# Two reorderings in a fused attention and GEGLU kernel: three up steps placed later, two weight loads placed earlier

## The chip, the cores and the metric

The kernel runs on one core of a Trainium2 chip. The metric is the time of one execution in microseconds as the device reports it; where several executions were made, their median is given. A profiled execution records when each instruction of each engine began and ended. Its *span* runs from the first to the last of them; the execution's time is somewhat longer than the span.

## The reference

One transformer block with its two branches side by side. Sequence 2048, width 448, 16 heads of 28, feed-forward width 1792; all inputs are bfloat16.

```python
def _A_ref(x, wqkv, wo):                      # sliding-window attention, W = 256
    qkv = ((x @ wqkv).reshape(B, S, 3, H, Dh)).transpose(2, 0, 3, 1, 4)
    q, k, v = qkv[0], qkv[1], qkv[2]
    scores = einsum("bhqd,bhkd->bhqk", q, k) * (Dh ** -0.5)
    mask = (i - j >= 0) & (i - j < 256)
    p = softmax(where(mask, scores, -1e9))
    return einsum("bhqk,bhkd->bhqd", p, v).transpose(0, 2, 1, 3).reshape(B, S, D) @ wo

def _B_ref(x, w_gate, w_up, w_down):
    return (gelu(x @ w_gate) * (x @ w_up)) @ w_down

xn = _layernorm(x)
return x + _A_ref(xn, ...) + _B_ref(xn, ...)
```

## The kernel before

**Blocks and stages.** The 2048 tokens are handled in four blocks of 512 (`qb` 0 to 3). Each block has two stages. In the first, `attention(qb, plan)` makes the scores of the block in ten *score steps*; in the second, `gated(...)` computes the gate and up products of the feed-forward branch. The ten score steps leave TensorE room, and a list written out by hand, `plan`, says what it does in each of them besides: plan[i] belongs to step i, counted from 0. So plan[5] is the sixth step, and plan[9] the last one.

**The fillers.** A filler is a Python generator, and `(u, 3)` in the plan means: draw three times from `u`, and each draw emits a piece of work. In block 3, `d = gen_down(2)` computes the output rows of block 2 (down projection and output projection, PSUM tiles `po`, one matmul over 448 columns for each draw) and `u = gen_up(3, (1, ..., 6), (4, 6))` computes up products of block 3 ahead of the second stage, for the pairs 1 to 6. A *pair* p is feature tiles p and p + 7. Each draw from `u` is one of seven *chunk steps* of a pair (`chunk`, L453): two matmuls of 64 rows by 512 columns, one in the upper and one in the lower half of the array. After the seventh step of a pair its two results are copied from PSUM (`ue`) to `hT` in SBUF: both by VectorE (L473), or one by VectorE and one by ScalarE for the pairs 4 and 6.

**A score step** (L640 to L678) does, in this order: at step 4 and step 6 the product with V of the heads of groups 0 and 1 (`pv`, PSUM tiles `ov`, L624), whose two halves are then copied by ScalarE (L608) and added up by VectorE (L609); the masks of the step before (VectorE, L572); the scores of this step (`sc`, L652); their exponential (ScalarE, L656); the plan's entries. "sums" and "inverse" in the plan belong to the softmax: VectorE transposes and takes reciprocals, and after an "inverse" GpSimd multiplies (L591). `pv` for groups 2 and 3 follows in the second stage, after gate pair 0.

**PSUM.** There are eight banks of 512 float32 columns. Four belong to the scores: in the first stage one tile `sc` of four banks (`score_pool(1)`), in the second two tiles `gt` of two banks for the gate (`score_pool(2)`). The other four, `b0` to `b3`, are single banks for everything else (`ue`, `u`, `po`, `ov`, `pq`, `pv`). They are handed out by a list:

```python
    def take(name, cols=QB, tag=None):
        tag = tag or spare[0]
        spare.remove(tag)
    ...
    def give(*tiles):
        for ps in tiles:
            spare.append(held.pop(id(ps))[0])
```

So the bank that has been in the list longest comes first. `give` stands where the code has emitted the last reader; the bank's next writer still waits until that reader has run. A draw that begins a pair takes two banks and holds them until the seventh step's copies.

**Block 3, the plan's steps around the change.** plan[0] and plan[1] draw 21 times from `u`: pairs 1, 2 and 3 whole. plan[2] to plan[4] draw from `d`. plan[5] draws once from `d`, which ends the output rows of two token tiles (L408 to L414, two `po` banks given back), then seven times from `u` (pair 4), and then three more times. plan[6], plan[7] and plan[8] draw from `d`, and plan[9] draws the rest of `u`.

**Block 0, loads.** Nearly all loads are issued from one queue, SyncE's. `ahead3` (L778) issues, in this order: four transposes and swaps of x, the gate columns of the pairs 0 to 2 (`load_ffn(wg, ..., slice(0, 3))`, two DMAs, one for each half of the array), the last four x tiles (L787), the up columns of the pairs 5 and 6 (two DMAs), the gate columns of the pairs 3 to 6 (two DMAs), then the output weights `wo` (L793, L794) and the down weights `wd` (L797). A new DMA of this queue waits for the completion of the eighth one before it, as they share eight semaphores in turn. The last four x tiles are first read in block 1, by `stat(12)` on VectorE. The gate columns of pair 3 are first read in block 0's second stage, by the fourth gate product, and the up columns of pair 5 by the only two up products that this stage has in block 0, those of the pairs 5 and 6 (pairs 0 to 4 were made ahead).

**ScalarE's queue in block 0's second stage** has the gelus of the gate pairs (L496), and between those of pairs 4 and 5 three DMA issues (`o_collect`, L351), which wait for GpSimd's multiplications.

Of the kernel before, what the change touches and what calls it, by code (L numbers as in the profile page):

```python
# [27 lines left out]
def kernel(  # L28
# [38 lines left out]
    wg = const.tile([P, 7, F // 2], bf16, name="wg")  # L67
    wu = const.tile([P, 7, F // 2], bf16, name="wu")
# [3 lines left out]
    def rows(w, c0, n):  # L72
        return w[c0 * P:(c0 + n) * P, :].rearrange("(c p) n -> p c n", p=P)

    def load_ffn(dst, w, pairs):

        wv64 = w.rearrange("(c p) (h n) -> p c h n", p=64, h=2)
        ns = slice(pairs.start * P, pairs.stop * P)  # L80
        for hi in range(2):
            nc.sync.dma_start(out=dst[64 * hi:64 * hi + 64, :, ns], in_=wv64[:, :, hi, ns])  # L82
# [25 lines left out]
    masks = const.tile([P, 3, 4, 64], bf16, name="masks")  # L108
# [56 lines left out]
    def norm(t):  # L165
        xn = work.tile([P, 4, P], bf16, name="xn", bufs=4)
        xf = xn[:, :, :].rearrange("p a b -> p (a b)")
        both = ((0, D, 0), (D, 64, 384))
        for lo, n, src in both if t > 3 else both[:1]:
            nc.vector.tensor_scalar(out=xf[:, lo:lo + n], in0=x_sb[:, t, src:src + n], scalar1=mv_all[:, t, 0:1],  # L170
                                    scalar2=rstd_all[:, t:t + 1], op0=ALU.subtract, op1=ALU.mult)
        xns[t] = xn

    def dma_transp(t):

        nc.sync.dma_start_transpose(out=xnT[:, :, t * P:(t + 1) * P], in_=xns.pop(t)[:, :, :].rearrange("p a b -> p (a b)"))
# [100 lines left out]
    def fill_pads(last):  # L277


        def put(dst, src, n, lo):  # L280

            src = src.rearrange("p (j d) -> p j d", d=Dh)[:, :, lo:]
            if n == 4:
                nc.gpsimd.tensor_copy(out=dst[:, 12:16, Dh:32], in_=src[:, :, 24:28])
            src = src[:, :, 0:24].rearrange("p j (g i) -> p g j i", i=8)[:, :, :, 0:4]
            nc.gpsimd.tensor_copy(out=dst[:, 0:12, Dh:32].rearrange("p (g j) i -> p g j i", j=4), in_=src)

        if not last:
            for c in range(3):
                k = wraw[:, c, D + 12 * Dh:2 * D]  # L290
                put(wqp[:, c, :, :], k, 4, 0)
                put(wkp[:, c, :, :], k, 3, 4)
            return
        put(w3p[0:64, :, :], w3k[0:64, :], 4, 0)
        put(w3p[64:128, :, :], w3k[64:128, :], 3, 4)
        nc.gpsimd.memset(w3p[64:128, 12:16, :], 0.0)
# [131 lines left out]
    def new_hT(qb):  # L428
        hT = blk.tile([P, NF, QB], bf16, name="hT", tag="hT")
        hTs[qb] = hT  # L430

    def swap(qb, t=None, n=4):

        t0 = P * (4 * qb if t is None else t)
        to = t0 - qb * QB + ring(qb).start
        for hi in range(2):
            nc.sync.dma_start(out=xsw[64 * hi:64 * hi + 64, :, to:to + n * P],
                              in_=xnT[64 - 64 * hi:P - 64 * hi, 0:3, t0:t0 + n * P])

    def swap_weights():  # L440

        for hi, src in enumerate((wqp, wkp)):
            nc.sync.dma_start(out=wsq[64 * hi:64 * hi + 64], in_=src[64 - 64 * hi:P - 64 * hi, 0:3])
# [334 lines left out]
    def ahead3():  # L778
        for t in (5, 6, 7):
            norm(t)  # L780
            dma_transp(t)
        swap(1, 4, 2)
        swap(1, 6, 2)
        fill_pads(False)
        swap_weights()
        load_ffn(wg, B_w_gate, slice(0, 3))
        nc.sync.dma_start(out=x_sb[:, 12:16, :], in_=xv[:, 12:16, :])  # L787
        load_ffn(wu, B_w_up, slice(5, 7))
        load_ffn(wg, B_w_gate, slice(3, 7))
        wo_v = A_wo.rearrange("(g j d) n -> j d g n", g=4, j=4)  # L790
        tail = A_wo[14 * Dh:, :].rearrange("(t i) n -> i t n", i=4)
        for j, (t0, n) in enumerate(SLOTS):
            nc.sync.dma_start(out=wo[32 * j:32 * j + Dh, 0:n, :], in_=wo_v[j][:, 0:n])  # L793
            nc.sync.dma_start(out=wo[32 * j + Dh:32 * j + 32, 0:n, :], in_=tail[:, t0:t0 + n])  # L794
        for k in range(0, NF, 4):
            n = min(4, NF - k)
            nc.sync.dma_start(out=wd[:, k:k + n, :], in_=rows(B_w_down, k, n))  # L797

    for qb in range(NB):
        if qb in (1, 3):  # L800
            tc.mark_branch_hint_location("general", hint="LikelyTaken",
                                         engines=[mybir.EngineType.DVE if qb == 1 else mybir.EngineType.PE])
        early = ()
        if qb == 0:
            new_hT(0)
            early = (0, 1, 2, 3, 4)
            u = chain(gen_qk((1, 2, 3), {1: (3, pvs[3]), 2: (2, pvs[2])}), gen_up(0, (1, 2, 3, 0, 4), (3, 4)))
            w = gen_pairs(1, (("v", 0), ("v", 2), ("k", 0), ("k", 1), ("k", 2)))
            plan = [[(u, 2), ahead, (u, 1)], [lambda: v_dense(2, pvs[2]), (u, 2), ahead2, (u, 1)],
                    [lambda: spare.append(spare.pop(1)), (u, 2), ahead3, (u, 4)], [lambda: stat(8), (u, 11)],  # L810
                    [lambda: stat(9), (u, 7), lambda: stat(10), (u, 7), lambda: fill_pads(True)], ["sums", (u, 7)],
                    ["inverse", "scale", (w, 11)], [(w, 10)],
                    [lambda: stat(11), (w, 7), lambda: rstd(8, 4), "sums", "inverse", (w, 7)]]
        else:
            d = gen_down(qb - 1)
            if qb < 3:
                u = gen_pairs(qb + 1, (("v", 0), ("k", 0), ("v", 2), ("k", 1), ("k", 2)))
                plan = [[(d, 14)], [(d, 11)], [(d, 11)], [(u, 7)], [(d, 18)], ["sums", (u, 7), "inverse"], [(u, 11)],
                        [lambda: q_last(qb + 1, nc.vector.tensor_copy), (d, 6), "sums"], [(d, 2), "inverse", (d, 10)],
                        [(u, 9), "masks", (u, 1)]]  # L820
                plan[3] = [(d, 1), (u, 7)]
                if qb == 2:
                    plan[0], plan[2] = [(d, 13)], [(d, 10)]
                if qb == 1:
                    for i, j in enumerate((0, 1, 2, 4)):
                        plan[j].insert(0, lambda t=12 + i: stat(t))
                    plan[4].append(lambda: rstd(12, 4))
                    plan[1] = plan[1][:1] + [lambda: q_last(1, nc.vector.tensor_copy), (d, 8)]
                    plan[2] = plan[2][:1] + [(d, 12), lambda: collect(1)]
                    plan[4].append(lambda: deliver(1))  # L830
            else:
                new_hT(3)
                early = (1, 2, 3, 4, 5, 6)
                u = gen_up(3, early, (4, 6))
                plan = [[(u, 12)], [(u, 9)], [(d, 12)], [(d, 10)], [(d, 12)], [(d, 1), (u, 7), "sums", (u, 3)], [(d, 12), "inverse"],
                        ["sums", "inverse", (d, 12)], [(d, 12)], [(u, 10), "masks", (u, 1)]]
        if qb in (1, 2):
            swap(qb + 1)
        score_pool(1)
        rest, after, flush = attention(qb, plan)  # L840
        nc.scalar.preload_act_table(ACT.Gelu_apprx_tanh)
        score_pool(2)
        if qb not in hTs:
            new_hT(qb)

        def hook(f):
            after(f)
            if qb in (1, 2) and f == 0:
                collect(qb + 1)
            if f == (8, 2, 2, 6)[qb]:  # L850
                o_collect(qb, nc.sync if qb else nc.scalar)
            if f == (12, 4, 4, 6)[qb]:
                o_deliver(qb)
                o_finish(qb)
            if qb == 0 and f == 6:
                nc.gpsimd.tensor_copy(out=wo[64:128, 3, :], in_=wo[0:64, 3, :])
            if qb in (1, 2) and f == 10:
                deliver(qb + 1)
            t = ({0: 8, 4: 9, 8: 10, 10: 11} if qb == 0 else {4: 12, 6: 13, 8: 14, 10: 15} if qb == 1 else {}).get(f)
            if t is not None:  # L860
                norm(t)
                dma_transp(t)

        gated(qb, early, rest, flush, hook)
        if qb < NB - 1:
            nc.scalar.preload_act_table_set("natural_log_exp_and_others")
# [156 lines left out]
```

## Time and profile before

| | us |
|---|---|
| median of 3 runs | 215.34 |
| lowest, highest | 215.28, 216.34 |
| profiled execution, its time | 216.02 |
| profiled execution, its span | 214.2 |
| TensorE matmul busy | 207.8 |
| VectorE, ScalarE, GpSimd busy | 157.7, 131.6, 48.6 |

The stages of the span, from the chain of waits: block 0's scores run to about 37.3 us, its gate and up products to 52.8, block 1 to 103.7, block 2 to 153.7. Block 3's score steps run from there to 183.0, its gate and up products to 196.5, and the last output rows to 210.4. The granted TensorE clock was 0.998 of full speed over the span.

In the views, PE is TensorE's matmuls, PEld its weight loads (which overlap the matmuls), DVE VectorE, ACT ScalarE, POOL GpSimd, SPq the queue of SyncE that issues DMAs. L456 is line 456. The chain of waits follows the work that ended last backwards: at each step to what released it, or to the instruction before it on the same engine. As long as it stays on PE, TensorE had no gap; where it leaves PE, TensorE waited. Ends of matmuls are modelled, so starts are the safer numbers.

### The profile page before, as it was taken

How to read it: one execution, taken by the hardware profiler on the slowest of the kernel's cores; microseconds unless marked ns; L12 is line 12 of the kernel's file. 1: busy time of each engine (PE TensorE's matmuls, PEld its weight loads, DVE VectorE, ACT ScalarE, POOL GpSimd, SP SyncE). 2: the span in 40 equal slices, each digit the busy share in tenths (PEclk: the TensorE clock that was granted, in tenths of full speed). 3: DMA queues.
4: the chain of work that ended last, by engine and by line, in shares of the span. 5: the costliest groups of instructions: out<-in, count | busy, mean ns of one | idle time of the engine just before them, and what ended most of it. 6: DMA issues, size and time to landing. Idle time of an engine off the chain costs nothing.

```text
span 214.2 us, 6428 instructions
## 1 busy us (share of the span) xinstructions
PE 207.8 (97%) x2722; PEld 101.9 (48%) x2722; DVE 157.7 (74%) x355; ACT 131.6 (61%) x123; POOL 48.6 (23%) x86
## 2 busy tenths in 40 slices
PE   7999999999999999999999999999999999999992
PEld 2433444445444445444445445444445444544992
DVE  7899988999767985796536987494483889569531
ACT  4699588555777977423777887523676776766000
POOL 5287658350100220041000211032000022006001
PEclk9999999999999999999999999999999999999999
DMA  6999579969410101003521001001000101000111
GB/s 186 267 218 230 107 169 238 215 199 214 109 47 26 42 16 29 8 5 65 74 73 46 24 0 30 19 0 34 12 3 3 44 3 42 9 0 0 26 44 49
DMA packets 23993, 15.67 MB, mean 73 GB/s; under 512 B 9208, under 2 KB 23832, under 8 KB 23960
## 3 DMA queue, kind: packets, MB, share of 16 engines
q1 hardware_dynamic: 22918, 14.87, 31.6%
q8 instruction: 22, 0.36, 0.7%
q10 hardware_dynamic: 1042, 0.34, 0.6%
q14 instruction: 11, 0.09, 0.2%
HBM read 9.26 MB, written 2.41 MB: 54 GB/s over the span
## 4 chain that ended last, share of the span: by engine, by line
PE 80%; DMA 6%; POOL 4%; ACT 3%; SPq 3%; issue 2%; DVE 2%; DVEq 0%; ACTq 0%; POOLq 0%
PE po L393 26%; PE gt L456 18%; PE u L456 12%; PE sc L652 5%; DMA wg<-in_B_w_gate_dram 5%; PE pq L334 4%; PE ue L456 4%; PE ov L624 4%; PE pv L320 3%; POOL p_sb L582 3%; SPq L82 2%; ACT p_sb L656 2%; DMA x_sb<-in_A_x_dram 1%; PE pq L191 1%; PE pv L191 1%
## 5 line engine op out<-in xcount | busy, mean ns | idle before, releaser
L656 ACT ACTIVATE p_sb<-sc 128x2048 bf16<-128x2048 f32 x39 | 73.2, 1878 | 21.0 <-PE sc L652 13.5
L496 ACT ACTIVATE p_sb<-gt 128x1024 bf16<-128x1024 f32 x28 | 28.7, 1024 | 34.2 <-PE gt L456 31.0
L591 POOL TENSOR_TENSOR oN<-oc,l 128x512 bf16<-128x512 f32 x16 | 21.5, 1353 | 121.3 <-DVE l L604 121.3
L393 PE MATMUL po<-wd,hT 128*128 128x448 bf16 (+1 forms) x266 | 46.2, 323 | 0.4 <-ACT oc L608 0.4
L456 PE MATMUL gt<-xnT,wg 64*128 64x512 bf16 x224 | 45.6, 376 | 0.0
L456 PE MATMUL gt<-xsw,wg 64*128 64x512 bf16 x168 | 39.6, 376 | 0.1
L504 DVE TENSOR_TENSOR hT<-p_sb,u 128x512 bf16<-128x512 bf16 x34 | 21.9, 677 | 16.3 <-PE u L456 16.1
L572 DVE TENSOR_TENSOR p_sb<-p_sb,masks 128x256 bf16<-128x256 bf16 (+1 forms) x90 | 27.8, 363 | 7.8 <-ACT p_sb L656 7.8
L393 PEld LDWEIGHTS <-hT 128*128 128x128 bf16 x266 | 24.6, 98 | 17.2 <-issue 2.8
L456 PEld LDWEIGHTS <-wg 64*128 64x128 bf16 x392 | 19.3, 94 | 22.8 <-DMA wg<-in_B_w_gate_dram 0.6
L456 PEld LDWEIGHTS <-wu 64*128 64x128 bf16 x392 | 19.2, 94 | 22.0 <-issue 0.8
L456 PE MATMUL u<-xnT,wu 64*128 64x512 bf16 x136 | 28.4, 376 | 0.0
L456 PE MATMUL u<-xsw,wu 64*128 64x512 bf16 x102 | 24.2, 376 | 0.0
L382 DVE TENSOR_TENSOR res<-po,x_sb 128x448 bf16<-128x448 f32 (+1 forms) x17 | 9.8, 592 | 12.1 <-PE po L393 9.8
L456 PE MATMUL ue<-xnT,wu 64*128 64x512 bf16 x88 | 18.0, 377 | 0.0
L456 PE MATMUL ue<-xsw,wu 64*128 64x512 bf16 x66 | 16.5, 377 | 0.0
L652 PE MATMUL sc<-qT,kT 28*64 28x320 bf16 (+7 forms) x648 | 16.4, 261 | 0.1
L582 POOL TENSOR_SCALAR_AFFINE_SELECT p_sb<-p_sb 128x512 bf16<-128x512 bf16 (+1 forms) x21 | 14.2, 701 | 6.6 <-ACT p_sb L656 6.5
L609 DVE TENSOR_TENSOR oc<-oc,ov 128x512 f32<-128x512 f32 x12 | 8.2, 686 | 9.3 <-ACT oc L608 9.3
L652 PEld LDWEIGHTS <-kT 28*64 28x64 bf16 (+1 forms) x648 | 7.5, 102 | 13.3 <-issue 12.0
L393 PE MATMUL po<-wo,oN 128*128 128x448 bf16 (+1 forms) x70 | 13.0, 320 | 0.0
L473 DVE CAST hT<-ue 128x512 bf16<-128x512 f32 x18 | 11.6, 679 | 1.3 <-PE ue L456 1.2
(108 smaller groups left out, 276.3 us busy)
## 6 DMA issues: line engine op xcount, KB each, us to landing
out_dram<-res SPq DMA_DIRECT2D x15, 112.0 KB
x_sb<-in_A_x_dram SPq DMA_DIRECT2D x3, 448.0 KB
wd<-in_B_w_down_dram SPq DMA_DIRECT2D x3, 448.0 KB
xsw<-xnT SPq DMA_DIRECT2D x6, 192.0 KB
wu<-in_B_w_up_dram SPq DMA_DIRECT2D x2, 560.0 KB
wg<-in_B_w_gate_dram SPq DMA_DIRECT2D x2, 448.0 KB
wg<-in_B_w_gate_dram SPq DMA_DIRECT2D x2, 336.0 KB
wraw<-in_A_wqkv_dram SPq DMA_DIRECT2D x2, 252.0 KB
```

The lines of the kernel that those rows point to most:

```text
L334: nc.tensor.matmul(ps, lhsT=w.rearrange("p h d -> p (h d)"), rhs=xchunk(qb, hi, c, qb * QB, QB), start=c == 0, stop=c == 6, tile_position= ...
L382: nc.vector.tensor_tensor(out=res[:, 0:w], in0=po[:, 0:w], in1=x_sb[:, t, lo:up], op=ALU.add)
L393: nc.tensor.matmul(po[:, a:b], lhsT=x[:, k, tt * P:(tt + 1) * P], rhs=wt[:, k, lo + a:lo + b], start=start and n == a == 0, stop=stop and ...
L456: nc.tensor.matmul(ps, lhsT=w[64 * hi:64 * hi + 64, c, p * P:(p + 1) * P], rhs=xchunk(qb, hi, c, qb * QB, QB), start=c == 0, stop=c == 6, ...
L473: copy(out=hTs[qb][:, p + 7 * i, :], in_=us[i])
L496: nc.scalar.activation(out=ges[p][:, :, :], in_=gt[:, :, :], func=ACT.Gelu_apprx_tanh)
L504: nc.vector.tensor_tensor(out=hT[:, p + 7 * i, :], in0=ge[:, i, :], in1=u, op=ALU.mult)
L572: nc.vector.tensor_tensor(out=reg, in0=reg, in1=m, op=ALU.mult)
L582: nc.gpsimd.affine_select(out=reg, in_=reg, pattern=mid + [[1 if diag else -1, min(w, P)]], compare_op=ALU.is_ge, fill=0.0, base=0 if diag ...
L591: nc.gpsimd.tensor_tensor(out=oN[:, g, :], in0=oc[:, :], in1=inv, op=ALU.mult)
L652: nc.tensor.matmul(ss[k0:k0 + nk, j, col:col + nq], lhsT=kT[r, g, kt * P + k0:kt * P + k0 + nk], rhs=qT[r, g, ring(qb).start + q0:ring(qb) ...
L656: nc.scalar.activation(out=p_sb[:, :, 0:ncol], in_=ss[:, :, 0:ncol], func=ACT.Exp, scale=SCALE)
```

## The change

In block 0, the two DMAs for the gate columns of pairs 3 to 6 and the two for the up columns of pairs 5 and 6 are issued ahead of the last four x tiles, in that order. In block 3, the three draws from `u` that began pair 5 in the sixth score step are made in the last score step. The order of the matmuls on TensorE differs at that one place; the sequence of VectorE's, ScalarE's and GpSimd's instructions is the same as before. In the changed program the first `po` after the seventh scores waits for VectorE instead of ScalarE.

```diff
         load_ffn(wg, B_w_gate, slice(0, 3))
+        load_ffn(wg, B_w_gate, slice(3, 7))
+        load_ffn(wu, B_w_up, slice(5, 7))
         nc.sync.dma_start(out=x_sb[:, 12:16, :], in_=xv[:, 12:16, :])
-        load_ffn(wu, B_w_up, slice(5, 7))
-        load_ffn(wg, B_w_gate, slice(3, 7))
         wo_v = A_wo.rearrange("(g j d) n -> j d g n", g=4, j=4)
...
                 u = gen_up(3, early, (4, 6))
-                plan = [[(u, 12)], [(u, 9)], [(d, 12)], [(d, 10)], [(d, 12)], [(d, 1), (u, 7), "sums", (u, 3)], [(d, 12), "inverse"],
-                        ["sums", "inverse", (d, 12)], [(d, 12)], [(u, 10), "masks", (u, 1)]]
+                plan = [[(u, 12)], [(u, 9)], [(d, 12)], [(d, 10)], [(d, 12)], [(d, 1), (u, 7), "sums"], [(d, 12), "inverse"],
+                        ["sums", "inverse", (d, 12)], [(d, 12)], [(u, 13), "masks", (u, 1)]]
```

## The prediction

> **What bounds the kernel now.** I read the page first, then the chain of waits, then the timeline of each engine around the two places that the diff touches, and last the DMA and SyncE views. Columns of the chain and the timeline: start in us, length in us, engine, what; in square brackets the idle time before it and what ended it.
>
> ```profile
> span 214.2 us, 6428 instructions
> ```
> ```profile
> PE 207.8 (97%) x2722; PEld 101.9 (48%) x2722; DVE 157.7 (74%) x355; ACT 131.6 (61%) x123; POOL 48.6 (23%) x86
> ```
>
> TensorE is busy for 97% of the span, and both edits leave its instructions as they are: the same matmuls, six of them at another place. So the time changes only by the moments at which TensorE stands still. In block 0 the chain of waits shows one:
>
> ```profile
> 33.45 10.12 DMA wg<-in_B_w_gate_dram
> 43.56 0.05 issue
> 43.61 4.70 PE gt L456 x41
> ```
> ```profile
> 42.66 0.80 PE L456 MATMUL gt<-xnT,wg 64*128 64x512 bf16 x4
> ```
>
> The chain leaves TensorE and runs back through the second half of gate columns 384 to 895 (pairs 3 to 6). The x4 row ends with the last two matmuls of gate pair 2 and the first of pair 3. In block 3, around the sixth and seventh score steps, the chain leaves TensorE twice:
>
> ```profile
> 170.02 0.69 DVE hT L473
> 170.71 0.04 issue
> 170.75 0.83 PE ov L624 x40
> ```
> ```profile
> 172.30 2.43 PE po L393 x12
> 174.73 0.35 PE sc L652 x16
> 175.09 2.38 PE po L393 x12
> ```
>
> The timeline has the weights of that `ov`, the scores behind it and the first `po` behind them:
>
> ```profile
> 170.55 0.79 PEld L624 LDWEIGHTS <-v_sb 64*32 64x32 bf16 x48 [0.42 <-issue]
> ```
> ```profile
> 171.43 0.43 PE L652 MATMUL sc<-qT,kT 28*64 28x320 bf16 x24
> ```
> ```profile
> 172.30 2.43 PE L393 MATMUL po<-wd,hT 128*128 128x448 bf16 x12 [0.45 <-ACT oc L608]
> ```
>
> A later row of the chain gives the beat:
>
> ```profile
> 183.03 1.51 PE gt L456 x14
> ```
>
> It is 14 half-height matmuls, seven chunk steps, in 1.51 us: 0.216 us a step. "Three half tiles" are three such steps, 0.65 us.
>
> **Block 0, the wait for gate weights.** After the x4 row two beats bring pair 3's first step to 42.66 + 0.43 = 43.09. Its second half runs at 43.61. The loss is 0.52 us, and the beat does not make it up.
>
> What lands when follows from the sizes of the transfers between 26 and 46 us (KB each) and from SyncE, whose issues wait for the eighth transfer before them: the five below for x, the two wu halves and the two wg halves, in turn. The last row is from the list of SyncE's waits.
>
> ```profile
> wg<-in_B_w_gate_dram SPq DMA_DIRECT2D x2, 448.0 KB
> wg<-in_B_w_gate_dram SPq DMA_DIRECT2D x2, 336.0 KB
> x_sb<-in_A_x_dram SPq DMA_DIRECT2D x1, 448.0 KB
> wu<-in_B_w_up_dram SPq DMA_DIRECT2D x2, 224.0 KB
> ```
> ```profile
> 37.56 0.25 SPq L794 DMA_DIRECT2D wo<-in_A_wo_dram  x1
> 38.45 0.32 SPq L793 DMA_DIRECT2D wo<-in_A_wo_dram  x1
> 39.66 0.25 SPq L794 DMA_DIRECT2D wo<-in_A_wo_dram  x1
> 41.75 0.32 SPq L793 DMA_DIRECT2D wo<-in_A_wo_dram  x1
> 43.58 0.25 SPq L794 DMA_DIRECT2D wo<-in_A_wo_dram  x1
> ```
> ```profile
> SPq L794 <- DMA x_sb<-in_A_x_dram: 0.3, 1, 0.3
> ```
>
> So the last x tiles had landed at about 37.5, both wu and both wg halves by 43.56: 2 x 224 + 2 x 448 = 1344 KB in 6.06 us, 222 KB per us. By that rate x took about 2.0 us and began at about 35.5. In the new order (estimates by that rate) wg lands at 37.5 and 39.5, wu at 40.5 and 41.5, x at 43.6. Needed: wg at 43.09, 3.6 us to spare. The two that are pushed back are needed here:
>
> ```profile
> 47.97 0.38 PE L456 MATMUL u<-xnT,wu 64*128 64x512 bf16 x1
> ```
> ```profile
> 53.97 0.62 DVE L155 BATCH_NORM_STATS2 st<-x_sb 128x6 f32<-128x448 bf16 x1
> ```
>
> Up pair 5 (47.45 after the shift) has 6 us to spare, the statistics of tile 12 ten. The five issues keep their places as a group, the bytes are the same, so the wo and wd loads behind them on SyncE's queue start as before. I price the delay at nothing; if its cover were gone, up pair 5 would wait, and gate 6 behind it on TensorE.
>
> The skill page "DMA: Bandwidth & Descriptors", section "Queues, rings and completion order", speaks against this step: completion is not in order per issuing engine, since up to 16 engines work at one row of rings. By it the order of issue need not be the order of landing, and this edit could bring nothing (the first rival). Here the five landings came one after the other in the order of issue, as the rows above show (37.56, 38.45, 39.66, 41.75, 43.58).
>
> What is late next, once 0.52 us are gone: ScalarE's gelus.
>
> ```profile
> 48.11 1.39 ACTq L351 DMA_DIRECT2D o<-oN  x3
> 49.60 1.02 ACT L496 ACTIVATE p_sb<-gt 128x1024 bf16<-128x1024 f32 x1 [1.68 <-DVE hT L501]
> 51.37 1.02 ACT L496 ACTIVATE p_sb<-gt 128x1024 bf16<-128x1024 f32 x1 [0.75 <-DVE hT L504]
> 52.41 1.28 ACT L866 ACT_TABLE_LOAD   x1
> 53.71 1.88 ACT L656 ACTIVATE p_sb<-sc 128x2048 bf16<-128x2048 f32 x1
> ```
> ```profile
> 55.88 0.43 PE L652 MATMUL sc<-qT,kT 28*64 28x320 bf16 x24
> ```
>
> Pair 5's gelu (49.60) stands behind three DMA issues on ScalarE's queue that wait for GpSimd, so it does not move. Pair 6's can move from 51.37 to 50.85, after 49.60 + 1.02 = 50.62: 0.23 us to spare. I take it that gate 6 releases it; the bracket names VectorE's product for pair 5 (started 50.66), and if that were so, the gelu, the table load and the exponential would stay, the exponential would end at 55.59, and the next score step (55.88) could come forward by only 0.29 us. So the gain is 0.29 to 0.52 us, and I take 0.52, because pair 6's buffer was pair 1's, read by VectorE long before.
>
> **Block 3, the moved steps.** Four single PSUM banks are handed out in turn, the longest free first. At the sixth score step the two `po` banks are given back, then up pair 4 takes the other two and gives them back. Before, pair 5's first three steps then take the `po` banks and hold them to the last score step. So pv(1) at the seventh step must take pair 4's banks, which VectorE copies until 170.02 + 0.69 = 170.71: its weights were loaded at 170.55, its matmul starts at 170.75, 0.20 us lost. Now no bank is left; the next `po` takes the bank that pv(1) filled, and waits 0.45 us for ScalarE's copy. From score to `po` is 175.09 - 174.73 = 0.36 us elsewhere; here it is 172.30 - 171.43 = 0.87, 0.51 us lost.
>
> After the edit pair 5 holds nothing there. pv(1) takes the two `po` banks, the next `po` takes pair 4's first bank, free by 170.71. Both waits fall away: 0.71 us. The three steps cost 0.65 us less in the sixth step and 0.65 us more in the last: sum nothing. They carry no DMA, no cast and no queue entry; pair 5's casts were in the last step anyway.
>
> What could be late next: the seventh step's exponential, which the eighth step's scores wait for, as one score tile holds all four other banks.
>
> ```profile
> 172.15 1.88 ACT L656 ACTIVATE p_sb<-sc 128x2048 bf16<-128x2048 f32 x1
> ```
>
> It ends 2.60 us after the scores' start at 171.43, and these steps then last 0.36 + 2.38 = 2.74 us: 0.14 us to spare. If the hand-over from ScalarE eats that, up to some 0.2 us come back (an estimate from those rows); the other end is nothing. I take nothing.
>
> In the last step VectorE now has pair 5's two casts, the last mask and pair 6's cast close together:
>
> ```profile
> 181.56 1.29 DVE L473 CAST hT<-ue 128x512 bf16<-128x512 f32 x2
> 182.76 0.82 DVE L572 TENSOR_TENSOR p_sb<-p_sb,masks 128x256 bf16<-128x256 bf16 x3
> 183.50 0.68 DVE L473 CAST hT<-ue 128x512 bf16<-128x512 f32 x1
> ```
>
> They sum to 2.79 us from about 1.6 us after the last scores, so end at 4.4. pv(3), which takes pair 6's banks, comes after 14 steps (3.02), gate 0 (1.51) and pv(2) (as pv(1), 171.43 - 170.75 = 0.68), at 5.2: 0.8 us to spare.
>
> **The sum.** 0.52 + 0.20 + 0.51 = 1.23 us. The profiled execution took 216.02 us, 1.82 of it around the span; it would take 214.8. It stands 0.68 us above the median of the runs, 215.34 (215.28 to 216.34), so from the median I get 214.1 us, 0.57% less.
>
> **The rivals.**
>
> (a) Block 0 gives nothing: the runs near 215.3 may not have the wait at all, as they are 0.68 us faster than the profiled one, which has it; or the order of issue does not carry over to landing. For: the spread of the runs, and a wait that hangs on DMA. Against: the landings in order. Only block 3 is left: 215.34 - 0.71 = 214.6 us.
>
> (b) Block 3 gives its gain back, since the exponentials take over as the bound of the seventh to ninth steps. For: 0.14 us of margin. Against: the fifth step has the same shape (pv, scores, copy, exponential, twelve `po`) without a wait. Only block 0 is left: 215.34 - 0.52 = 214.8 us.
>
> (c) Slower: VectorE's queue in the last score step. Three masks of that kind took more than twice as long earlier:
>
> ```profile
> 174.26 1.86 DVE L572 TENSOR_TENSOR p_sb<-p_sb,masks 128x256 bf16<-128x256 bf16 x3
> 174.51 1.46 POOL L591 TENSOR_TENSOR oN<-oc,l 128x512 bf16<-128x512 f32 x1 [24.64 <-DVE l L604]
> ```
>
> If the whole queue is slowed by that ratio (1.86 to 0.82), 2.79 us become 6.3, end at 7.9, and pv(3) waits 2.7 us: 215.34 - 1.23 + 2.7 = 216.8 us. It decides from 3.6 us of queue on, and eats the whole gain at 4.8. Against: that slow mask ran beside a GpSimd multiplication, these come with "inverse", and none of those stands in the last two steps. The skill page "SBUF — State Buffer", section "Who interferes with whom", has the rule: a VectorE instruction with two SBUF inputs contends with a GpSimd instruction that reads SBUF. The mask above, with two SBUF inputs, agrees (1.86 us beside the GpSimd row); by the rule the casts, which read PSUM alone, would not be slowed so, and the queue would be 2.79 + 1.04 = 3.8 us at most.
>
> (d) The edits do nothing, because both waits only change their name: 215.3 us.
>
> **Chances.** Forecast 0.52, (a) 0.24, (b) 0.12, (c) 0.05, (d) 0.07. Half a per cent, about what a measurement of this kernel can tell from no change, is 1.08 us: below 214.26 is faster. The forecast lies 0.15 us inside that line, and its own range is 213.6 to 214.5 us; I put 0.46 of its 0.52 below the line, and 0.03 of (a), where the wait is shorter but there. Faster 0.49, within 0.45, slower 0.06 (c and a little of d). The range reaches over (a) and (b) and leaves out (c) and most of (d): 213.5 to 215.2 us; its low end is for runs in which the wait in block 0 is twice as long.
>
> **What would show it.** Right: the weight loads of gate pair 3 in block 0 follow on without a wait for wg, and pair 3's steps keep the beat; pv(1) in block 3 starts with its weights, and the `po` after the seventh scores 0.36 us behind them, with no ScalarE copy in the chain; the last score step holds 14 up steps, and gate 0 follows without a gap. Wrong: a wait of TensorE for wu at up pair 5 or for ScalarE at a score step from the seventh on; pv(3) waiting for a VectorE cast; or, for (a), a profile without the wait in block 0 and a time that stays at 214.6.

## The result and the profile after

The changed kernel takes 214.60 us in the median of 12 runs (214.23 to 215.06), the kernel before 215.22 us (12 runs, 214.95 to 216.34): ratio 0.9966, 95% interval 0.9951 to 0.9981, so 0.4 to 1.1 us less. That is rival (a)'s time. The two profiled executions are further apart than the medians: 216.02 us before, 214.79 after, a difference of 1.23 us. That it is the prediction's sum to the last digit is partly chance: in the chains, the last addition of output rows starts 1.17 us earlier (209.21 against 210.38), and the spans differ by 1.1.

First the chain of waits of the changed kernel around the gate products of block 0 (start, length, engine and what):

```profile
37.58 1.51 PE gt L456 x14
39.09 1.10 PE ov L624 x36
40.19 7.66 PE gt L456 x70
47.85 1.51 PE u L456 x14
49.36 1.51 PE gt L456 x14
50.87 1.51 PE u L456 x14
52.38 0.35 PE sc L652 x16
```

The chain stays on TensorE from gate pair 0 to block 1's first scores; before, it left TensorE at pair 3 for the gate weights. The five gate products from pair 1 on are one stretch of 70 matmuls at the beat. The first scores of block 1 and of block 3 stood here in the chain of the kernel before:

```profile
52.84 0.35 PE sc L652 x16
153.79 0.35 PE sc L652 x16
```

Block 3's stand here in the changed kernel:

```profile
153.32 0.35 PE sc L652 x16
```

Block 1 starts at 52.38 instead of 52.84, 0.46 us earlier, and block 3 at 153.32 instead of 153.79, 0.47 earlier: what was gained here was still there a hundred us later. Gate pair 0 had begun 0.07 us later than in the kernel before (37.42 against 37.35 in the timeline), so the step itself gave 0.53 us.

SyncE's queue in the same profile, the issues that wait for the moved loads:

```profile
37.14 0.31 SPq L794 DMA_DIRECT2D wo<-in_A_wo_dram  x1
38.87 0.32 SPq L793 DMA_DIRECT2D wo<-in_A_wo_dram  x1
39.87 0.25 SPq L794 DMA_DIRECT2D wo<-in_A_wo_dram  x1
40.87 0.32 SPq L793 DMA_DIRECT2D wo<-in_A_wo_dram  x1
42.45 0.25 SPq L794 DMA_DIRECT2D wo<-in_A_wo_dram  x1
```

They waited for the two wg halves, the two wu halves and x, in turn. The issues of one queue stand in order in any case; what shows a landing is the idle time of the queue before an issue. The first row has none (the issue before it ended at 37.10), so the first half was there by 37.14, perhaps long before. The other four have 0.7 to 1.4 us each, and so those four landed in the order of issue. The second wg half was there by 38.87 us; the estimate was 39.5. ScalarE's gelus of pairs 5 and 6 and the table load behind them:

```profile
49.67 1.02 ACT L496 ACTIVATE p_sb<-gt 128x1024 bf16<-128x1024 f32 x1 [2.21 <-DVE hT L501]
50.91 1.02 ACT L496 ACTIVATE p_sb<-gt 128x1024 bf16<-128x1024 f32 x1 [0.22 <-PE gt L456]
51.95 1.28 ACT L866 ACT_TABLE_LOAD   x1
```

Pair 5's gelu did not move (49.60 before), pair 6's came forward by 0.46 and is now put down to gate 6. So VectorE's product was not its releaser, as the prediction took it.

The chain in block 3, from the sixth score step to gate pair 0:

```profile
167.70 0.29 PE po L410 x2
168.00 1.51 PE ue L456 x14
169.51 0.66 PE ov L624 x40
170.17 0.36 PE sc L652 x16
170.52 2.39 PE po L393 x12
172.91 0.35 PE sc L652 x16
173.27 2.37 PE po L393 x12
175.64 0.35 PE sc L652 x16
176.00 2.38 PE po L393 x12
178.37 0.34 PE sc L652 x16
178.72 3.14 PE ue L456 x28
181.86 1.51 PE gt L456 x14
```

No VectorE cast and no ScalarE copy stand in it any more, and `po` follows 0.35 us behind the seventh scores. From block 3's first scores to gate pair 0 it is 181.86 - 153.32 = 28.54 us; before, 183.03 - 153.79 = 29.24. The difference is 0.70 us, where the prediction had 0.71.

So in the profiles both steps came true in full. The question is why the medians show only half of the sum (0.62 of 1.23 us).

### The profile page after: what moved, and what is told of

Read it like the earlier page. It is cut to its first block, busy times and chain, and to the rows that moved or that the text cites. A ratio compares the mean times of both kernels' runs of the same rounds, so it can differ in the third digit from the quotient of the medians.

```text
span 213.1 us, 6428 instructions
## 1 busy us (share of the span) xinstructions
PE 207.6 (97%) x2722; PEld 101.2 (47%) x2722; DVE 157.5 (74%) x355; ACT 131.6 (62%) x123; POOL 48.6 (23%) x86
## 4 chain that ended last, share of the span: by engine, by line
PE 94%; DVE 1%; ACT 1%; DMA 1%; issue 1%; DVEq 0%; ACTq 0%
PE po L393 26%; PE gt L456 20%; PE u L456 12%; PE ue L456 8%; PE pq L334 7%; PE sc L652 6%; PE ov L624 5%; PE pv L320 4%; PE pq L191 2%; PE pv L191 1%; DMA x_sb<-in_A_x_dram 1%; ACT p_sb L656 1%; DVE st L155 1%; PE s L191 1%; PE pk L191 1%
## 5 line engine op out<-in xcount | busy, mean ns | idle before, releaser
L456 PE MATMUL gt<-xsw,wg 64*128 64x512 bf16 x168 | 40.7, 376 | 0.0
L456 PEld LDWEIGHTS <-wu 64*128 64x128 bf16 x392 | 18.7, 94 | 22.4 <-issue 0.8
L456 PE MATMUL u<-xsw,wu 64*128 64x512 bf16 x102 | 24.7, 376 | 0.0
```

The source lines that it names most:

```text
L456: nc.tensor.matmul(ps, lhsT=w[64 * hi:64 * hi + 64, c, p * P:(p + 1) * P], rhs=xchunk(qb, hi, c, qb * QB, QB), start=c == 0, stop=c == 6, ...
```

## The experiments

Eight kernels, in two groups of four; within a group they share one chip and its runs of the kernel before (35 in the first group, median 215.38; 33 in the second, median 215.42). The theory: (A) both waits are in every execution, and something takes block 0's part back; or (B) block 0's wait is only in some executions, the profiled one among them. Ratios are against the kernel before, with the 95% interval.

**e1: only block 0.**

```diff
+        load_ffn(wg, B_w_gate, slice(3, 7))
+        load_ffn(wu, B_w_up, slice(5, 7))
         nc.sync.dma_start(out=x_sb[:, 12:16, :], in_=xv[:, 12:16, :])
-        load_ffn(wu, B_w_up, slice(5, 7))
-        load_ffn(wg, B_w_gate, slice(3, 7))
```

> Only the block 0 edit: gate columns of pairs 3 to 6 and up columns of pairs 5 and 6 issued ahead of the last x tiles; block 3 as before. Theory A (the wait for gate weights in the profile of before, 0.52 us, is in the ordinary runs too): 0.5 us less than before, 214.7 where before is 215.2, and no wait of TensorE for wg in the trace. Theory B (the ordinary runs mostly lack that wait, so that the edit removes something only some runs have): 0 to 0.2 us less in the median, but fewer runs above 215.5.

Measured: 215.09 us, ratio 0.9997 (0.9987 to 1.0007): no difference that can be told, and a gain of at most 0.3 us. The ratio is not the quotient of the two medians, which would be 0.9987, 0.29 us less; but the unchanged kernel, run again (e5), also comes out 0.24 us below the median of its group, so 0.29 is no proof of a gain. None of e1's 12 runs is above 215.5 us; of the 35 runs of before, 13 are. Its trace has no wait for wg. So theory A's 0.5 us is out; B's two statements fit, the first by the ratio only.

**e2: only block 3.**

```diff
-                plan = [..., [(d, 1), (u, 7), "sums", (u, 3)], ..., [(u, 10), "masks", (u, 1)]]
+                plan = [..., [(d, 1), (u, 7), "sums"], ..., [(u, 13), "masks", (u, 1)]]
```

> Only the block 3 edit: three up steps from the sixth to the last score step; loads as before. Theory A (two bank waits of 0.20 and 0.51 us go, in every run): 0.7 us less than before, 214.5 where before is 215.2, with pv(1) starting at its weights and po 0.36 us behind the seventh scores. Theory B (block 3 gives part of it back in ordinary runs): 0.1 to 0.4 us less. If e1 gives 0 and this gives 0.6 to 0.7, block 0 is what fell short in the change.

Measured: 214.39 us, ratio 0.9960 (0.9943 to 0.9978), 0.5 to 1.2 us less. It has the old order of loads, and yet its chain of waits in block 0 looks like that of the changed kernel:

```profile
37.38 1.51 PE gt L456 x14
38.90 1.10 PE ov L624 x36
39.99 7.66 PE gt L456 x70
```

There was no wait for wg to remove. SyncE's last two issues that wait for the wg halves show why:

```profile
39.98 0.32 SPq L793 DMA_DIRECT2D wo<-in_A_wo_dram  x1
42.08 0.25 SPq L794 DMA_DIRECT2D wo<-in_A_wo_dram  x1
```

Here the second half had landed by 42.08, and pair 3 needs it two products after 39.99, at 43.0. In the profile of before the same row stood at 43.58.

**e3: both, once more.**

> The changed kernel once more, beside the two halves on the same chip. If the halves add up: the sum of e1 and e2. By the earlier runs 0.6 us less than before (ratio 0.997); by the prediction's sum 1.2 us less.

Measured: 214.57 us, ratio 0.9967 (0.9955 to 0.9978). That is e2's time. Of the two halves, block 3 is the whole of what can be measured.

**e4: one of the three steps left in the sixth score step.**

```diff
-                plan = [..., [(d, 1), (u, 7), "sums", (u, 3)], ..., [(u, 10), "masks", (u, 1)]]
+                plan = [..., [(d, 1), (u, 7), "sums", (u, 1)], ..., [(u, 12), "masks", (u, 1)]]
```

> Loads as before; two of the three up steps of pair 5 moved to the last score step, one left in the sixth, so that pair 5 still holds its two banks from there on. Theory A (what counts is that pair 5 holds banks, not how much work stands in the sixth step): pv(1) still waits for pair 4's casts, now 0.63 us instead of 0.20, and po still 0.51 us; the moved steps cost 0.43 us in the last step and save nothing in the sixth: 0.4 us more than before. Rival (less filler in the sixth step is what helps, in proportion): two thirds of e2's gain, 0.4 to 0.5 us less than before.

Measured: 215.70 us, ratio 1.0026 (1.0013 to 1.0039): 0.3 to 0.8 us slower. Two thirds of the work were moved, and the time went the other way. The timeline at pv(1) and behind it:

```profile
170.10 0.74 PE L624 MATMUL ov<-p_sb,v_sb 64*32 64x256 bf16 x48 [0.56 <-DVE hT L473]
```
```profile
171.65 1.67 PE L393 MATMUL po<-wd,hT 128*128 128x448 bf16 x8 [0.45 <-ACT oc L608]
```

TensorE reaches pv(1) earlier and waits longer for pair 4's cast; behind the scores it waits for ScalarE's copy as in the kernel before. The one step is enough to hold the two banks. It is the banks, not the amount of work.

**e5: the kernel before, once more, with a trace of its own.**

> The kernel before, once more, with a trace of its own. Both theories: ratio 1.000 within the interval, which is the control for the others. Theory B (wg lands late only in some executions): this trace has no wait of TensorE for wg, as those of e2 and e4, which have the same loads; wg lands about 0.7 us before pair 3 needs it, with some 0.4 us of scatter. Theory A (the wait is in the kernel's ordinary execution, and what the block 0 edit gains is lost elsewhere): the trace has the wait of about 0.5 us again.

Measured: 215.18 us, ratio 0.9991 (0.9972 to 1.0009). The control holds. Its trace has no wait for wg:

```profile
40.09 7.66 PE gt L456 x70
```
```profile
42.20 0.25 SPq L794 DMA_DIRECT2D wo<-in_A_wo_dram  x1
```

The wg half landed by 42.20 and was needed at 43.1. The two bank waits of block 3 are in it as in the first profile (cast, `ov`, copy, `po` in the chain; the short rows between them are left out):

```profile
169.46 0.69 DVE hT L473
170.19 0.83 PE ov L624 x40
171.10 0.59 ACT oc L608
171.74 2.43 PE po L393 x12
```

**e6 and e7: the gate weights made to land later**, with one down-weight load issued ahead of them (224 KB, or 448 KB); the same load is left out of its old place.

```diff
         load_ffn(wu, B_w_up, slice(5, 7))
+        nc.sync.dma_start(out=wd[:, 12:14, :], in_=rows(B_w_down, 12, 2))
         load_ffn(wg, B_w_gate, slice(3, 7))
...
-        for k in range(0, NF, 4):
+        for k in range(0, 12, 4):
```

That is e6; e7 has `wd[:, 0:4, :]` from `rows(B_w_down, 0, 4)` there, and its loop is `range(4, NF, 4)`.

> The kernel before with one 224 KB down-weight load (the last two tiles of w_down) issued ahead of the gate columns of pairs 3 to 6, so that these land about 1.0 us later (224 KB at 222 KB per us). Theory B (ordinary slack about 0.7 us): about 0.3 us more than before, 0.1 to 0.5. Theory A (the wait is ordinary, 0.5 us, and each us of delay counts): 1.0 us more. Rival C (waits in block 0 are absorbed later and never reach the end): no change.

> The same with a 448 KB down-weight load (the first four tiles) ahead, about 2.0 us later. Theory B: 2.0 - 0.7 = about 1.3 us more than before, and the trace shows a wait of TensorE for wg of that size, carried to the end of the span. Theory A: 2.0 us more. Rival C: no change in the time though the wait is there.

Measured: e6 215.46 us, ratio 1.0007 (0.9989 to 1.0026); e7 216.78 us, ratio 1.0051 (1.0024 to 1.0079), 0.5 to 1.7 us slower. e6 rules out theory A's 1.0 us and leaves B and C; e7 rules out C, and its interval ends below A's 2.0. In e7's profiled execution the second wg half landed at 45.26, and TensorE's weight loads and the chain say:

```profile
45.28 1.62 PEld L456 LDWEIGHTS <-wg 64*128 64x128 bf16 x18 [2.08 <-DMA wg<-in_B_w_gate_dram]
```
```profile
45.29 4.70 PE gt L456 x41
```

A wait of 2.1 us, and the span is 215.4 us against e5's 213.2: it reaches the end undiminished. Two of e7's ten runs took 215.47 us, level with the kernel before, so in some executions the wait may be short or missing even here; these were not traced. A wait for wg costs its full length when there is one. With the order of loads of the kernel before, it is in one of five traces (the first profile; not in e2, e4, e5 and e8), and even the later load of e6 met none (its 70 gate matmuls follow on at 40.21).

**e8: the three steps put behind the seventh score step's `po`, not into the last step.**

```diff
-                plan = [..., [(d, 1), (u, 7), "sums", (u, 3)], [(d, 12), "inverse"], ...]
+                plan = [..., [(d, 1), (u, 7), "sums"], [(d, 12), "inverse", (u, 3)], ...]
```

> Loads as before; the three up steps of pair 5 moved from the sixth to the end of the seventh score step instead of the last, behind its twelve po steps. Theory (it is the two banks that pair 5 holds while pv(1) and the next po ask for theirs): the same gain as e2, 0.7 us less than before (ratio 0.996 to 0.997), with pv(1) starting at its weights and po 0.36 us behind the scores. Rival (what helped is the longer last step, which covers the last exponential or the casts): no gain, 215.2.

Measured: 214.69 us, ratio 0.9965 (0.9946 to 0.9985), the same gain as e2. In its chain the waits are gone and the three steps stand behind `po`:

```profile
169.47 0.66 PE ov L624 x40
170.12 0.36 PE sc L652 x16
170.48 2.39 PE po L393 x12
172.87 0.75 PE ue L456 x6
```

The last score step is as short as before the change here, so its length is not what helped. Both places tried behind the `po` that follows pv(1) do it.

No variant beats the changed kernel by more than the intervals; e2 (214.39) is level with it.

## Why the prediction was right in its mechanisms and half a microsecond off

The sum gave 214.1 us, and 214.60 was measured. The prediction's range, 213.5 to 215.2 us, holds that time because it was drawn over rival (a) as well, and not because the sum was right.

- **Block 3, two bank waits, 0.71 us.** Right, in mechanism and size: 0.70 us in the profiles, 0.5 to 1.2 us in e2's runs. e4 and e8 show that holding the two banks is the cause.
- **Moved steps cost nothing.** Right: the last step's `ue` went from 2.50 to 3.14 us, the sixth's lost as much, and the gate product follows without a gap.
- **Block 0, 0.52 us.** This is the step that failed, by its size: "0.52 + 0.20 + 0.51 = 1.23 us ... so from the median I get 214.1". The mechanism was right, and 0.46 us were gained against that profiled execution. But its 0.52 us were taken off the median as if every run had them. e1 gives 0.06 us (a gain of at most 0.3), and four further traces with the old order of loads (e2, e4, e5, e8) have no wait. The rival (a) named this, from the 0.68 us between the profiled execution and the median, and got a chance of 0.24; after these traces it would have the larger one. That its argument held is partly luck, since only a part of that distance is the wait (see below). Of the 35 and 33 runs of before in the two groups (214.70 to 216.56), only two and three are as slow as the first profile's 216.02 us.
- **Order of landing.** Right: the second wg half, both wu halves and x landed in the order of issue; up pair 5 (47.85) and the statistics of tile 12 (53.69 us, x there by 42.45) did not wait.
- **Gelus.** Right: pair 6's moved by 0.46, ended at 50.91 + 1.02 = 51.93, 0.45 us before block 1's first scores in the chain (52.38), and TensorE did not wait for it.
- **Rival (b), exponentials as the bound.** Did not happen: the eighth scores follow the `po` in the chain at 172.91.
- **Rival (c), VectorE in the last step.** Did not happen: gate pair 0 and pv(2) and pv(3) follow at the beat, and the mask between the casts took 0.82 us as before.
- **Rival (d), the waits change their name only.** Did not happen: the ratio's interval ends at 0.9981.

That the edit in block 0 removes the times above 215.5 us (none of e1's 12 runs, 13 of 35 before) is not shown: with block 3's edit in place, the runs with it (e3, 214.20 to 215.05) and without it (e2, 214.19 to 215.18) look alike.

Nor is a long time by itself the mark of that wait. The first profiled execution took 1.02 us longer than e5's (216.02 against 215.00). Of this, 0.56 us are there at block 1's first scores (52.84 against 52.28), nearly all of it the wait. The rest came at the end. The last addition of output rows stands in the chains of the first profile, of e5 and of e8 as follows; their spans are 214.2, 213.2 and 213.4 us.

```profile
210.38 0.39 DVE res L382
```
```profile
209.82 0.39 DVE res L382
```
```profile
209.27 0.39 DVE res L382
```

From there to the end of the span it is 3.8, 3.4 and 4.1 us. e8's profiled execution had no wait for wg and still took 215.10 us where its median was 214.69. What lengthens this last stretch was not tried.

## What to carry to other kernels

Before a wait for a DMA is priced from one profile, see where that execution stands among the runs: if it lies far above their median, the wait may be one that most executions do not have, and its removal need not move the median. The one time alone does not settle it, as here only about half of the excess was the wait; a second trace of the same kernel (e5) does more. The waits between engines on the core recurred in all six traces that have them (the first profile, e1, e4, e5, e6, e7): from pair 4's first step to `ov` 2.28 or 2.29 us, from `ov` to `po` 1.55. Such a wait can be priced from one trace. Filler work that spans several stages of a plan holds its buffers for all of that time; ask who takes the next buffer in between, and start the filler behind him.

## What was not expected of the hardware

With the same order of loads, the second wg half had landed by 42.08, 42.20, 42.97 and 43.58 us in four executions (e2, e5, e8 and the first profile). SyncE's queue had issued the wg pair at 31.72, 31.93, 32.47 and 32.77, in the same order; e4 (31.30, landed by 42.35) breaks it. So in those four most of the 1.5 us of scatter (1.05 us) was there before the load set out, and the trips themselves differ by 0.8 us (10.3 to 11.1). SyncE's queue in the timelines of the kernel before (the first profile), and of e2:

```profile
30.13 1.28 SPq L787 DMA_DIRECT2D x_sb<-in_A_x_dram  x1
31.45 1.28 SPq L82 DMA_DIRECT2D wu<-in_B_w_up_dram  x2
32.77 1.84 SPq L82 DMA_DIRECT2D wg<-in_B_w_gate_dram  x2
```
```profile
29.73 0.62 SPq L787 DMA_DIRECT2D x_sb<-in_A_x_dram  x1
30.40 1.28 SPq L82 DMA_DIRECT2D wu<-in_B_w_up_dram  x2
31.72 1.97 SPq L82 DMA_DIRECT2D wg<-in_B_w_gate_dram  x2
```

The issue of x took 1.28 us in the one and 0.62 in the other, and the queue was 0.40 us later already when it came to x; together that is the 1.05 us by which wg was issued later. Why an issue takes twice as long was not tried. e2 and e4 were taken on one chip and e5 and e8 on another; the chip of the first profile is not on record, so that it has a part in the late landing is not excluded.

The delay by a load put ahead was not in proportion: 224 KB moved the landing from 42.20 to 42.71, 448 KB to 45.26. One trace each, and a landing scatters by up to 1.5 us.
